# Two buffers for two output tiles and two-tap products in the tail of an SSM and gated-MLP gradient

## The chip, the cores and the metric

The kernel runs on one core of a Trainium2 chip. The metric is device time in microseconds of one execution. A profile of one execution gives the times of the single instructions. The engines are PE (matrix products; PEld is its weight load), DVE (elementwise on 128 lanes), ACT (copies out of PSUM, activations), POOL, and SP, whose queue issues nearly all DMAs. PSUM is the memory that PE writes, SBUF the one where tiles live.

## The reference

The forward pass takes `x = q` of shape (1, 2048, 512), normalises each row, and returns `x + A + B`. `A` convolves `k` with a short filter of 4 taps per channel, multiplies with `v`, runs a long causal convolution of length 2048 by FFT, and multiplies with the normalised rows. `B` is a bilinear gated MLP of hidden size 1376.

```python
def _A_ref(q, k, v, shift_k, ssm_k, ssm_D):
    for t in range(ks):
        k_shift = k_shift + k_pad[:, t:t + S, :] * shift_k[:, ks - 1 - t][None, None, :]
    kv = k_shift * v
    ...
    y = y + kv * ssm_D[None, None, :]
    return q * y
def _B_ref(x, w_gate, w_up, w_down):
    h = g * u
    return jnp.einsum("bsf,fd->bsd", h, w_down)
xn = _layernorm(x, axis=-1)
return x + _A_ref(xn, A_k, A_v, ...) + _B_ref(xn, B_w_gate, ...)
```

The kernel returns the forward result (`out_0`) and nine gradients for a given `grad_out`: of q (`out_1`), k (`out_2`), v (`out_3`), the short filter (`out_4`), the long filter (`out_5`), its skip weight (`out_6`), and the three MLP weights (`out_7` to `out_9`).

## The kernel before

A sequence of 2048 rows lies in SBUF as 128 partitions with R = 16 rows each, 512 channels (D) in bf16. The first part (to about 300 us) does the layer norm, the transforms of the long convolution and the MLP's forward and backward products over 8 chunks of 256 rows, and leaves intermediate results in DRAM (`HDD`, `GD`, `KS`, `BX`, `XN`).

The change lies in the last part. Its main loop is `dw()`, which forms the three MLP weight gradients in 11 blocks of hidden units. `down_grad(fb)` accumulates `pd` over 16 rows (L1014) and stores `od`; for the last block ACT copies one half of `od` and DVE the other, and each half is stored by its own queue (L1027). `pu` (L1050) is copied to `og` and stored (L1061). In between, `hid_t` transposes the hidden activations `hb` loaded from `HDD`; the last three blocks come through transposing DMAs instead (`natT`, L808).

Beside `dw()` run four generators, each advanced every second or third step of `dw()`:

- `inv_y()` brings 4 rows at a time back from the transform: `yC`, the convolution's result, and `dd`. From `dd`, DVE forms `dks = dd * v` (L950) and the gradient of v (L951). `dd` has two buffers in the pool `c2b`.
- `dsk_gram()` forms the gradient of the short filter as products of `dks` with shifted `k` in PSUM (`pk`), masks them with the identity into `kd` (L1079) and reduces them (L1081). A last small transpose gives `dskt`. `kd` and `dskt` have one buffer each in the pool `c2`.
- `inv_dk()` forms the gradient of the long filter, `o5t`, stored at L996.
- `ew()` walks over a list of 16 pieces: `final(0)`, `final(1)`, `bwd(0)`, `final(2)`, `bwd(1)`, ..., `final(7)`, `bwd(6)`, `bwd(7)`. Each piece works on 2 of the 16 rows, so on tiles of 128 x 1024. Before each piece, `put_late()` stores what earlier pieces left in the list `late` (L1167).

`final(b)` forms the result `o` (L1125, L1126) and the gradient of q, `e` (L1129 to L1141), with `bb` loaded from `BX` and a scratch tile `dxn` in fp32. `o`, `e` and `dxn` have one buffer each. `bwd(b)` forms the gradient of k, `dk` (two buffers), as a sum over 4 taps: products of `dks`, shifted by the tap, with the filter row `skb` (L1103, L1105), and sums (L1106). Its scratch tile `tk` shares the single buffer of `dxn`.

The order of instructions on each engine is not written out: a planner takes the operations in the order in which the program lists them as priority, works out with a cost model when each would be ready, and fixes one order for each engine and for each queue that issues DMAs. A block marked `high_priority` goes ahead when ready. An operation that needs a buffer waits until the tile before it in that buffer is done with, its store included. On the chip each engine, and the SP queue, then works strictly in that order. The PSUM tag `p2` has three buffers; `pt`, `pq`, `pu`, `pk` and `po` share them.

Of the kernel before, what the change touches and what calls it, by code (L numbers as in the profile page):

```python
# [8 lines left out]
BF = mybir.dt.bfloat16  # L9
F32 = mybir.dt.float32  # L10
I32 = mybir.dt.int32
ALU = mybir.AluOpType
# [6 lines left out]
D = 512  # L19
F = 1376  # L20
R = 16
P = 128
NC4 = 4
# [167 lines left out]
def kernel(  # L191
# [24 lines left out]
    nc = tc.nc  # L216
# [20 lines left out]
    def dve(o, i):  # L237
        nc.vector.tensor_copy(o, i)  # L238
# [13 lines left out]
    def P2(name, shape, dt=F32):  # L252
        return ps2.tile(shape, dt, name=name, tag="p2")

    def P1(name, shape, dt=F32):
        return ps1.tile(shape, dt, name=name, tag="p1")
# [5 lines left out]
    skb = const.tile([P, 4, D], BF, name="skb")  # L262
# [642 lines left out]
    c2b = ctx.enter_context(tc.tile_pool(name="c2b", bufs=2, side="right", reuse_waits="tile"))  # L905
    c2 = ctx.enter_context(tc.tile_pool(name="c2", bufs=1, side="right", reuse_waits="tile"))
    yC = c2.tile([P, R, D], BF, name="yC")
    dks = c2.tile([P, R + 3, D], BF, name="dks")
# [158 lines left out]
    def dsk_gram():  # L1067
        for c in range(NC4):
            pk = P2("pk", [P, 2, D])
            for r in range(R):  # L1070
                for h in range(2):
                    c0 = c * 128 + 64 * h
                    nc.tensor.matmul(pk[64 * h:64 * h + 64, h, 0:256], lhsT=dks[:, r, c0:c0 + 64],  # L1073
                                     rhs=KH[0][:, r:r + 4, c0:c0 + 64], start=(r == 0), stop=(r == R - 1))
            kd = c2.tile([P, 4, 64], F32, name="kd")
            with tc.high_priority(offset=SOON):
                for h in range(2):
                    hs = slice(64 * h, 64 * h + 64)
                    nc.vector.tensor_tensor(kd[hs], pk[hs, h, 0:256].rearrange("q (j c) -> q j c", j=4),  # L1079
                                            ident[hs, hs].unsqueeze(1).to_broadcast((64, 4, 64)), op=ALU.mult)  # L1080
                nc.vector.tensor_reduce(dsk[:, c, :], kd[:], axis=AX.X, op=ALU.add)  # L1081
            yield
        dskb = c2.tile([P, 4, NC4], BF, name="dskb")
        nc.vector.tensor_copy(dskb[:], dsk[:].rearrange("q c i -> q i c"))
        for _ in range(2):
            yield
        pt = P1("pts", [P, 4, P], BF)
        for j in range(4):
            nc.tensor.transpose(pt[:NC4, j, :], dskb[:, 3 - j, :], ident[:])
        dskt = c2.tile([NC4, P, 4], BF, name="dskt")  # L1090
        dve(dskt[:], pt[:NC4].rearrange("c j q -> c q j"))
        nc.sync.dma_start(out_4.rearrange("(c p) j -> c p j", p=128), dskt[:])
        yield

    def bwd(b):
        rb = slice(2 * b, 2 * b + 2)
        dk = c2b.tile([P, 2, D], BF, name="dk")
        t = c2.tile([P, 2, D], BF, name="tk", tag="dxn")
        for j in range(4):
            src = dks[:, 2 * b + j:2 * b + j + 2, :]  # L1100
            w = skb[:, j:j + 1, :].to_broadcast((P, 2, D))
            if j == 0:
                nc.vector.tensor_tensor(dk[:], src, w, op=ALU.mult)  # L1103
            else:
                nc.vector.tensor_tensor(t[:], src, w, op=ALU.mult)  # L1105
                nc.vector.tensor_tensor(dk[:], dk[:], t[:], op=ALU.add)  # L1106
        late.append((o2_n[:, rb, :], dk))

    FL = {}
# [2 lines left out]
    def load_fin(b):  # L1112
        bb = c2b.tile([P, 2, 2, D], BF, name="bb")
        nc.sync.dma_start(bb[:], BX[:, 2 * b:2 * b + 2, :, :])
        FL[b] = bb

    def final(b):
        if b + 1 < 8:
            load_fin(b + 1)
        bb = FL.pop(b)  # L1120
        rb = slice(2 * b, 2 * b + 2)
        tt = nc.vector.tensor_tensor
        stt = nc.vector.scalar_tensor_tensor
        o = c2.tile([P, 2, D], BF, name="o0")
        tt(o[:], xnC[:, rb], yC[:, rb], op=ALU.mult)  # L1125
        tt(o[:], o[:], bb[:, :, 0, :], op=ALU.add)  # L1126
        late.append((o0_n[:, rb, :], o))
        e = c2.tile([P, 2, D], BF, name="e")
        tt(e[:], goC[:, rb], yC[:, rb], op=ALU.mult)  # L1129
        dxn = c2.tile([P, 2, D], F32, name="dxn")  # L1130
        for i in range(2):
            r = 2 * b + i
            stt(dxn[:, i], e[:, i], 1.0, bb[:, i, 1, :], op0=ALU.mult, op1=ALU.add, accum_out=s1[:, r:r + 1])
            stt(e[:, i], dxn[:, i], 1.0, xnC[:, r, :], op0=ALU.mult, op1=ALU.mult, accum_out=s2[:, r:r + 1])
        nc.vector.tensor_scalar(m2[:, rb], s2[:, rb], -1.0 / D, None, op0=ALU.mult)
        stt(m1[:, rb], s1[:, rb], -1.0 / D, rstd[:, rb], op0=ALU.mult, op1=ALU.mult)
        for i in range(2):
            r = 2 * b + i
            stt(dxn[:, i], xnC[:, r, :], m2[:, r:r + 1], dxn[:, i], op0=ALU.mult, op1=ALU.add)
            nc.vector.tensor_scalar(e[:, i], dxn[:, i], rstd[:, r:r + 1], m1[:, r:r + 1], op0=ALU.mult, op1=ALU.add)  # L1140
        tt(e[:], e[:], goC[:, rb], op=ALU.add)  # L1141
        late.append((o1_n[:, rb, :], e))
# [16 lines left out]
    for b in range(8):  # L1159
        tail.append(lambda b=b: final(b))  # L1160
        if b > 0:
            tail.append(lambda b=b: bwd(b - 1))
    tail.append(lambda: bwd(7))

    def put_late():
# [16 lines left out]
    def load_dk():  # L1182
        gks.append(load_gk(0))
        gks.append(load_gk(1))
        yield

    sides = [every(seq(inv_y(), load_dk()), 0, 3), every(dsk_gram(), 27, 2), every(inv_dk(), 35, 3), every(ew(), 10, 3)]
    for n, _ in enumerate(dw()):
        for sd in sides:
# [36 lines left out]
```

## Time and profile before

| what | value |
|---|---|
| median of three runs | 489.96 us |
| lowest, highest | 488.36, 490.24 us |
| the profiled execution | 488.56 us |
| its span, first to last instruction | 486.8 us |
| mean granted PE clock | 0.995 |
| PE busy | 471.5 us (97%) |
| DVE busy | 342.0 us (70%) |
| ACT busy | 310.1 us (64%) |

The span and the time of the same execution differ by 1.8 us, which lie around it. Busy shares are means over stages of different kinds. Below, a line of a timeline gives the start, the duration, the engine (SPq is the queue of SP), the line of the kernel, the operation, the tile written and the tiles read, and their sizes.

### The profile page before, as it was taken

To read this page: it belongs to the slowest core of one execution; us is meant where nothing else is said; L and a number is where in the kernel's file an instruction comes from. 1 tells how busy PE (TensorE), PEld (TensorE's weight loads), DVE (VectorE), ACT (ScalarE), POOL (GpSimd) and SP (SyncE) were. 2 spreads that over 40 slices of the span, in tenths; PEclk is the share of its full clock that TensorE was granted. 3 is DMA by queue.
4 is the path that set the end of the run, shared out by engine and by line. 5 is a ranking of instruction groups with operands and counts; after the bars stand their busy time and mean duration, and the time that the engine had idled before them with its cause. 6 is when DMAs were issued, how large, how long until landed. Compare 5 with 4: busy or idle time off the path is not lost.

```text
span 486.8 us, 10509 instructions
## 1 busy us (share of the span) xinstructions
PE 471.5 (97%) x4335; PEld 314.8 (65%) x4335; DVE 342.0 (70%) x625; ACT 310.1 (64%) x351; POOL 13.9 (3%) x30
## 2 busy tenths in 40 slices
PE   8998999999999999999999999999999999999992
PEld 7867755547647457357357734577677778777790
DVE  7889989988275667677687874021260999998895
ACT  4956677669568678789689954567557523733320
POOL 8000000000000000000000000020000000000000
PEclk9999999999999999999999999999999999999997
DMA  8999999889999978788977199989999797999518
GB/s 266 373 366 362 314 261 359 295 314 323 306 293 284 247 235 246 240 257 250 296 231 238 63 366 324 369 314 348 342 368 373 286 354 248 316 310 231 186 48 293
DMA packets 105837, 139.87 MB, mean 287 GB/s; under 512 B 33435, under 2 KB 78912, under 8 KB 104126
## 3 DMA queue, kind: packets, MB, share of 16 engines
q1 hardware_dynamic: 104206, 137.85, 86.9%
q10 hardware_dynamic: 1584, 1.36, 1.0%
q8 instruction: 34, 0.56, 0.5%
q14 instruction: 13, 0.11, 0.1%
HBM read 68.45 MB, written 63.41 MB: 271 GB/s over the span
## 4 chain that ended last, share of the span: by engine, by line
PE 76%; DMA 11%; DVE 10%; ACT 1%; issue 1%; DVEq 0%; SPq 0%; ACTq 0%
PE px L555 14%; PE pgu L512 13%; PE pu L1050 12%; PE py L548 7%; PE pd L1014 6%; PE pdh L518 6%; PE pt L847 4%; PE pq L920 3%; PE ps L584 3%; DMA ssk<-in_A_ssm_k_dram 3%; PE pg L613 3%; PE pf L370 2%; DMA out_dram<-e 2%; DMA x_b<-in_A_q_dram 2%; PE pk L1073 2%; DMA XN<-x_b 1%
## 5 line engine op out<-in xcount | busy, mean ns | idle before, releaser
L555 PE MATMUL px<-WT,hd 128*128 128x512 bf16 (+1 forms) x352 | 81.0, 380 | 0.0
L1050 PEld LDWEIGHTS <-xnC 128*128 128x128 bf16 x704 | 67.1, 98 | 8.8 <-issue 0.9
L555 PEld LDWEIGHTS <-hd 128*128 128x128 bf16 (+1 forms) x352 | 32.8, 98 | 44.4 <-issue 7.7
L1050 PE MATMUL pu<-natd,xnC 128*128 128x256 bf16 x512 | 58.5, 273 | 0.2 <-ACT nath L235 0.2
L235 ACT CAST gu<-pgu 128x1024 bf16<-128x1024 f32 (+1 forms) x48 | 45.4, 946 | 16.5 <-PE pgu L512 16.3
L235 ACT CAST GO<-pg 128x1024 bf16<-128x1024 f32 x48 | 46.2, 1015 | 13.8 <-issue 7.2
L235 ACT CAST SP<-ps 128x1024 bf16<-128x1024 f32 x47 | 45.6, 1025 | 13.7 <-PE ps L584 11.8
L600 DVE TENSOR_TENSOR T<-SP 128x2048 bf16<-128x2048 bf16 x24 | 29.4, 1223 | 34.8 <-ACT SP L235 34.7
L512 PE MATMUL pgu<-xt,Wu 128*128 128x256 bf16 (+1 forms) x352 | 53.1, 273 | 0.7 <-DVE kn L238 0.6
L512 PE MATMUL pgu<-xt,Wg 128*128 128x256 bf16 (+1 forms) x352 | 52.8, 273 | 0.2 <-DMA Wg<-in_B_w_gate_dram 0.2
L518 PE MATMUL pdh<-gt,WdT 128*128 128x256 bf16 (+1 forms) x352 | 46.9, 273 | 0.2 <-ACT WdT L235 0.2
L235 ACT CAST fst<-pf 128x1024 bf16<-128x1024 f32 x44 | 42.7, 1030 | 5.7 <-ACT fst L235 2.1
L512 PEld LDWEIGHTS <-Wu 128*128 128x128 bf16 (+1 forms) x352 | 33.0, 100 | 15.0 <-issue 10.1
L548 PE MATMUL py<-Wd,hd 128*128 128x512 bf16 (+1 forms) x176 | 41.4, 380 | 0.0
L235 ACT COPY natd<-pt 128x2048 bf16<-128x2048 bf16 x16 | 30.0, 1874 | 14.1 <-PE pt L847 14.1
L235 ACT CAST og<-pu 128x1024 bf16<-128x1024 f32 (+1 forms) x11 | 10.9, 993 | 43.1 <-PE pu L1050 38.5
L518 PEld LDWEIGHTS <-WdT 128*128 128x128 bf16 (+1 forms) x352 | 34.8, 100 | 5.0 <-ACT WdT L235 0.4
L512 PEld LDWEIGHTS <-Wg 128*128 128x128 bf16 (+1 forms) x352 | 34.8, 100 | 4.1 <-DMA Wg<-in_B_w_gate_dram 0.5
L533 DVE TENSOR_TENSOR hd<-gu,dh 128x1024 bf16<-128x1024 bf16 (+1 forms) x48 | 30.9, 643 | 0.8
L532 DVE TENSOR_TENSOR hd<-gu 128x512 bf16<-128x512 bf16 (+1 forms) x48 | 19.1, 398 | 15.9 <-ACT gu L235 15.9
L1014 PE MATMUL pd<-goC,nath 128*128 128x512 bf16 x128 | 30.1, 379 | 0.0
L548 PEld LDWEIGHTS <-hd 128*128 128x128 bf16 (+1 forms) x176 | 16.5, 98 | 20.8 <-issue 3.1
(176 smaller groups left out, 693.2 us busy)
## 6 DMA issues: line engine op xcount, KB each, us to landing
HDD<-hd SPq DMA_DIRECT2D x35, 384.0 KB, 5.8
FD<-fst SPq DMA_DIRECT2D x24, 512.0 KB, 5.5
X<-FD SPq DMA_DIRECT2D x24, 512.0 KB, 5.2
GD<-GO SPq DMA_DIRECT2D x24, 512.0 KB, 3.9
g<-GD SPq DMA_DIRECT2D x11, 1024.0 KB, 8.7
hb<-HDD SPq DMA_DIRECT2D x8, 1344.0 KB, 7.9
bb<-BX SPq DMA_DIRECT2D x8, 512.0 KB, 6.2
BX<-bx SPq DMA_DIRECT2D x7, 512.0 KB, 3.9
```

The source lines that it names most:

```text
L235: nc.scalar.copy(o, i)
L512: nc.tensor.matmul(pgu[:w, i, t, :], lhsT=W[:, c, f0:f0 + w], rhs=xt[:, :, c, :], start=(c == 0), stop=(c == NC4 - 1))
L518: nc.tensor.matmul(pdh[:w, i, :], lhsT=WdT[:, c, f0:f0 + w], rhs=gt[:, :, c, :], start=(c == 0), stop=(c == NC4 - 1))
L532: nc.vector.tensor_tensor(hd[:fw, fb0:fb0 + n, 0, :], gu[:fw, :n, 0, :], gu[:fw, :n, 1, :], op=ALU.mult)
L533: nc.vector.tensor_tensor(hd[:fw, fb0:fb0 + n, 1:3, :], gu[:fw, :n], dh[:fw, :n].unsqueeze(2).to_broadcast((fw, n, 2, 256)), op=ALU.mult)
L548: nc.tensor.matmul(py[:], lhsT=hd[:fw, fb, 0, ss], rhs=Wd[:fw, fb, :], start=(fb == 0), stop=(fb == NFB - 1))
L555: nc.tensor.matmul(px[:], lhsT=hd[:fw, fb, t, ss], rhs=W[:fw, fb, :], start=(t == 1 and fb == 0), stop=(t == 2 and fb == NFB - 1))
L584: nc.tensor.matmul(ps[32 * q:32 * q + 32, a, :], lhsT=TB.EF[64 * a:64 * a + 64, 4 * g + q, ri].rearrange("p k j -> p (k j)"), rhs=X[64 * a ...
L600: tt(W[:].rearrange("p c a d -> p c (a d)"), A[:, i:i + 1].rearrange("p c a d -> p c (a d)").to_broadcast((P, 2, 2 * D)), B[:].rearrange(" ...
L847: nc.tensor.transpose(pt[:, r, :fw], hs[:, (r % 2) * 128:(r % 2) * 128 + 128], ident[:fw, :fw])
L1014: nc.tensor.matmul(pd[:fw, :], lhsT=nat_h(fb, r), rhs=goC[:, r, :], start=(r == 0), stop=(r == R - 1))
L1050: nc.tensor.matmul(pu[:, c, :, :fw], lhsT=xnC[:, r, cs(c)], rhs=nat_d(fb, r), start=(r == 0), stop=(r == R - 1))
```

## The change

It has three parts.

1. `o0` and `e` get two buffers each, so `final(b + 1)` can write its tiles while those of `final(b)` are still being stored. That takes two more tiles of 2 KB in each partition.
2. `kd` and `dskt`, 1 KB each, no longer have places of their own: they take turns in the two buffers of `dd`, which are also used by the last `og1`.
3. `bwd` forms the products of two taps in one operation of 2048 elements. Its source is a pattern over `dks` with two windows of two rows, the second shifted by one row, so that the middle row is read twice; the filter rows are repeated over the window. `tk` doubles to [P, 2, 2, D] in bf16, as large as `dxn`, whose buffer it shares. The four taps are summed by three additions as before.

```diff
-            kd = c2.tile([P, 4, 64], F32, name="kd")
+            kd = c2b.tile([P, 4, 64], F32, name="kd", tag="dd")
...
-        dskt = c2.tile([NC4, P, 4], BF, name="dskt")
+        dskt = c2b.tile([NC4, P, 4], BF, name="dskt", tag="dd")
...
-        t = c2.tile([P, 2, D], BF, name="tk", tag="dxn")
-        for j in range(4):
-            src = dks[:, 2 * b + j:2 * b + j + 2, :]
-            w = skb[:, j:j + 1, :].to_broadcast((P, 2, D))
-            if j == 0:
-                nc.vector.tensor_tensor(dk[:], src, w, op=ALU.mult)
-            else:
-                nc.vector.tensor_tensor(t[:], src, w, op=ALU.mult)
-                nc.vector.tensor_tensor(dk[:], dk[:], t[:], op=ALU.add)
+        t = c2.tile([P, 2, 2, D], BF, name="tk", tag="dxn")
+        for j in (0, 2):
+            s = dks[:, 2 * b + j:2 * b + j + 3, :]
+            (part, row, elem) = s.ap
+            src = bass.AP(s.tensor, s.offset, [part, [row[0], 2], [row[0], 2], elem])
+            w = skb[:, j:j + 2, :].unsqueeze(2).to_broadcast((P, 2, 2, D))
+            nc.vector.tensor_tensor(t[:], src, w, op=ALU.mult)
+            nc.vector.tensor_tensor(dk[:], t[:, 0] if j == 0 else dk[:], t[:, 1 if j == 0 else 0], op=ALU.add)
+            if j:
+                nc.vector.tensor_tensor(dk[:], dk[:], t[:, 1], op=ALU.add)
...
-        o = c2.tile([P, 2, D], BF, name="o0")
+        o = c2.tile([P, 2, D], BF, name="o0", bufs=2)
...
-        e = c2.tile([P, 2, D], BF, name="e")
+        e = c2.tile([P, 2, D], BF, name="e", bufs=2)
```

## The prediction

> **What bounds the kernel now.** I read the table of stages first (busy time of each engine in stretches that I chose), then the waits of PE, then DVE in order of time, then the sync queue at the end. In the stages, each line gives a stretch and the busy us of PE, PEld, DVE, ACT and POOL in it, the granted clock, the DMA share and GB/s:
>
> ```profile
> 360.00:380.00 20.00, 20.00 (x176) 14.94 (x174) 5.40 (x10) 11.80 (x11) 0.00 (x0) 1.00 0.99 370
> 380.00:400.00 20.00, 20.00 (x219) 15.52 (x218) 19.20 (x44) 8.33 (x7) 0.00 (x0) 1.00 0.86 298
> 400.00:420.00 20.00, 20.00 (x234) 16.16 (x232) 19.57 (x41) 9.70 (x8) 0.00 (x0) 1.00 0.88 306
> 460.00:478.00 18.00, 17.09 (x170) 14.60 (x167) 16.60 (x32) 4.75 (x6) 0.00 (x0) 1.00 0.36 132
> 478.00:486.80 8.80, 0.00 (x0) 0.00 (x0) 3.21 (x6) 0.00 (x0) 0.00 (x0) 0.70 0.84 259
> ```
>
> The reader is to see two things. PE is full at full clock until its last matmul, which starts at 476.49 and lasts 0.59, so ends at 477.08; then 9.7 us pass without it. And DVE, which this change touches, is a quarter busy from 360 to 380 and full from 380 on: it is late from then to the end. PE itself hardly waits; of PE after 300 us the list of waits has one line:
>
> ```profile
> PE pu L1050 <- ACT nath L235: 0.2, 1, 0.2
> ```
>
> DVE in order of time (start, us, instruction, and in brackets the idle time in front of it with its cause):
>
> ```profile
> 358.15 0.69 DVE L1141 TENSOR_TENSOR e<-e,goC 128x1024 bf16<-128x1024 bf16 x1
> ...
> 361.70 0.69 DVE L951 TENSOR_TENSOR kb<-dd,kb 128x1024 bf16<-128x1024 bf16 x1
> 376.91 0.69 DVE L1125 TENSOR_TENSOR o<-xnC,yC 128x1024 bf16<-128x1024 bf16 x1 [14.53 <-DMA out_dram<-o]
> ...
> 452.29 0.69 DVE L1129 TENSOR_TENSOR e<-goC,yC 128x1024 bf16<-128x1024 bf16 x1 [3.29 <-DMA out_dram<-e]
> ```
>
> So `final(1)` stands 14.53 us, with its inputs there, until the store of `final(0)`'s `o` has landed and frees the one buffer; `e` does the same later. The lateness reaches the end through the sync queue:
>
> ```profile
> 476.69 0.33 SPq L1167 DMA_DIRECT2D out_dram<-dk  x1
> 477.11 1.04 SPq L1061 DMA_DIRECT2D out_dram<-og  x2
> 478.24 1.37 SPq L996 DMA_DIRECT2D out_dram<-o5t  x2
> 481.05 0.33 SPq L1167 DMA_DIRECT2D out_dram<-dk  x1
> 481.47 1.77 SPq L1061 DMA_DIRECT2D out_dram<-og  x2
> 483.33 0.58 SPq L1027 DMA_DIRECT2D out_dram<-od  x1
> ```
>
> The queue issues in order. It stands at the store of `dk` until DVE has computed it, and the stores of `og` (whose copy on ACT began at 467.50), of `o5t` (copied by 469.42) and of the last `og` (474.47) stand behind it. DVE's half of `od` is also queued on DVE behind `bwd(7)`: it runs at 480.94, while ACT's half ran at 477.17. From the end of the last issue (483.91) to the end of the span are 2.9 us.
>
> **Part 1, two buffers for `o` and `e`.** It removes DVE's waits on their stores: 14.53 us for `o`, and 5.08 for `e` (0.59, 0.31, 3.29, 0.89 by DVE's order of time); another 1.0 us of waits for `dk`'s store stays. What is late next? `final(1)` can start at 362.3: yC's rows are there, `bb` for it was issued at 354.80 and lands 4.8 to 7.3 us later, by 362.1. From its first to its last operation `final` takes about 7.3 us of DVE (four of 0.60, four of 0.61, 1.33 and 0.92 for the two pairs, 0.2 for the small ones), `bwd(0)` behind it some 4.7. `final(2)` again needs `o`'s first buffer, whose store was issued at 365.19 and, by the 10.2 us that is the longest landing of an `o`, is down at 375.4. So of the 14.53 us, 7.3 + 4.7 = 12.0 are filled and 2.5 remain as a wait. If `e`'s 5.08 go too, DVE gains 17.1 us; if they come back as waits on the second buffer, 12.0. Nothing in the trace shows a loss here, but an idle engine in the stage 360 to 380 is also all there is to gain from: 14.6 us is the ceiling there.
>
> The stores of `final(1)` and `bwd(0)` move with it, 3 x 256 KB, into the stretch with DMA share 0.99. At that stretch's 370 GB/s they are 2.1 us of transfer, ahead of loads of `hb` that must be there for the transposes. The load issued at 366.89 took at most 13.9 us (the longest landing of an `hb`), so is down at 380.8; its transposes start on PE at 384.0. I take 0 with 3.2 us as the cover; without it, each us late is a us of PE.
>
> **Part 2, `kd` and `dskt` in `dd`'s two buffers.** The operations stay: 8 of 0.42, 4 of 0.41, one of 0.68. The new wait is on the last readers of `dd` (start 387.73, done 388.4); `kd` is first written at 393.28. That is 4.9 us of cover. Behind a late `kd` stand the three PSUM buffers of tag p2, and with them PE. `og1`, the last user of `dd`, is written at 473.67, long after `dskt`'s store (issued 433.85). Two `kd` buffers instead of one gain nothing: no wait names `kd`. I take 0; from the rows, between 0 and the 4.9 us by which `dd`'s readers could slip unnoticed.
>
> **Part 3, products of two taps in one operation.** Per `bwd` before: 4 products and 3 sums, seven operations of 1024 elements. Each of the chained ones starts 0.725 after the one before (473.00, 473.73, 474.45), the others 0.60: 0.60 + 6 x 0.725 = 4.95 alone, 7 x 0.60 = 4.2 in between other work. After: 2 products of 2048 and 3 sums. A product of 2048 with a broadcast input lasts 1.22 (T<-SP, L600), and its follower starts 1.14 later where it does not depend on it. Chained: 2 x 1.25 + 3 x 0.725 = 4.68; in between: 2 x 1.14 + 3 x 0.60 = 4.08. The gain is 0.12 to 0.27 per `bwd`, for eight 1 to 2.2 us; I take 1.6. The early start of the first product (two `dk` at 329.11, when DVE was idle) is lost, since it now needs the buffer shared with `dxn`: 2 x 0.60, so 0.4 is left.
>
> The unsure piece is the source pattern: two windows of two rows that overlap by one row. The nearest row is hd<-gu,dh, L533: three free dimensions with a repeated one, 1024 elements in 688 ns, the pace of the plain ones. I take that pace. The other bound is one element at a time, the pace of rows with fp32: 256 elements 0.42, 512 elements 0.69, so 0.27 for each 256 more, and 2048 in 2.31. It would add 2 x 1.09 to each `bwd`, 17.4 us in all. The Trainium skill, page "Vector Engine (DVE) Microarchitecture Reference", section 5.1, states that a two-source operation goes two elements per cycle when every operand is 16-bit with an innermost step of 1, and that it lists input rows that overlap among what was not measured. By its condition the sum stays 4.68 and 4.08; L533's row agrees, and no run here shows overlapping rows.
>
> **The sum.** DVE's chain: 12.0 + 5.1 + 0.4 = 17.5 us earlier at its end (12.4 if `e`'s waits come back). It ended with `bwd(7)` at 480.94; it would end at 463.4 to 468.5. All of it beyond 3.9 us lies beside PE, which ends at 477.08 as before. So the end is set by PE: ACT's half of `od` done at 477.54, DVE's at 477.6 (0.41), the sync queue free by then, its issue 0.58, and 2.9 to the end: 481.1. ACT's half was issued at 478.96, 1.4 after its copy, by a wait that the list does not name; if that stays, 479.32 + 2.9 = 482.2. I take the middle, 481.6: 5.2 less than the span of 486.8. The profiled execution took 488.56, so 483.4; the three runs have a median of 489.96, 1.4 above it, which gives 484.8. I say 484.0.
>
> **Rivals.**
> *The tail is given back in part (about 490).* The instruction order is planned anew, and every stall of PE goes straight to the end, since PE has no slack at all. A stall of 3 to 5 us takes the gain. For it: the gram's weight loads at 389.25 waited 0.21 for DVE, so PE already starts the gram at the moment `dks` is written. If DVE stands in `final(2)` then, up to 7.3 us come in front, of which some 3 hurt. Against it: `dks`' last load was issued at 377.20, lands 6.3 later, 383.5, and today's order has them late too. Time 487.5 to 492.
>
> *Slower (494).* One mechanism: the sync queue stops at a store of `e` that DVE has not yet computed, now placed further ahead, with the load of `hb` behind it. The longest such stop is 5.9 us now; one `final` and one `bwd` between two `e` make 12.0. Less the 3.2 of cover, PE stands 8.8 us; with the tail's 5.2 gained, that is 489.96 + 3.6 = 493.6. It decides from a stop of 10.8 us on (3.2 + 5.2 + 2.45). For it: the queue waited 20.6 us for `e` in all. Against it: those waits come from the lateness that goes.
>
> *The wide products run at one element per cycle.* DVE then ends 17.4 us later than forecast: at 481 instead of 463.4, or 486 instead of 468.5. The first is no change in the tail (489.96), the second 5 us more (495).
>
> **How the numbers follow.** A measurement of this kernel tells 0.5% (2.45 us) from no change. The forecast's mechanism has 0.60, with 481.5 to 487.4 as its own range; the gain given back 0.17; the queue's stop 0.15; slow products 0.08, of which half stays within 0.5% and half is slower. Faster 0.61 with a little of the given-back case, same 0.20, slower 0.19. To leave out no more than 2 in 10 the range must take in the middle case and the first of the slow ones: 481.5 to 493.
>
> **What would show it.** Right: no idle time in front of L1125 between 362 and 377; DVE's last `dk` before 472; DVE's half of `od` within 0.6 us of ACT's; the last og stores issued by 476.5; PE ending near 477; the wide product at 1.22. Wrong: PE's idle time after 300 above 3 us, with `hb`, `dd` or `dks` as its cause; a wide product near 2.3; a wait at `bb` in place of `o`'s.

## The result: faster by 1.4%

The changed kernel takes 481.98 us (median of 4 runs, 481.83 to 482.23), the kernel before 489.16 in the same comparison (median of 4). The ratio is 0.986, with a 95% interval of 0.983 to 0.989. The forecast was 484.0, faster, within 481.5 to 493.0. The profiled execution after took 482.23 us with a span of 480.4, 6.4 less than the span before.

The stages after, with the busy us of PE, PEld, DVE, ACT and POOL, the granted clock, the DMA share and GB/s:

```profile
360.00:380.00 20.00, 20.00 (x173) 14.70 (x171) 14.70 (x27) 11.80 (x11) 0.00 (x0) 1.00 0.97 360
380.00:400.00 20.00, 20.00 (x220) 15.44 (x218) 19.72 (x43) 8.32 (x7) 0.00 (x0) 1.00 0.89 322
400.00:420.00 20.00, 19.79 (x231) 15.82 (x230) 19.65 (x40) 9.16 (x8) 0.00 (x0) 1.00 1.03 371
460.00:478.00 18.00, 17.03 (x169) 14.53 (x166) 7.93 (x10) 4.74 (x6) 0.00 (x0) 1.00 0.58 196
478.00:481.00 3.00, 0.00 (x0) 0.00 (x0) 0.00 (x0) 0.00 (x0) 0.00 (x0) 0.81 0.14 33
```

From 360 to 380 DVE went from 5.40 to 14.70 us of work; from 460 to 478 from 16.60 to 7.93. PE is unchanged: 17.03 us in the second last line against 17.09. What shrank is the stretch behind PE, 9.7 us before and 3.4 now. (The last window reaches 0.6 us past the end of the span.)

DVE after in order of time, with idle time and its cause in brackets. These are the three longest waits between 360 and PE's end, the last product and sums of `bwd(7)`, and its half of `od`:

```profile
365.88 0.69 DVE L1127 TENSOR_TENSOR o<-o,bb 128x1024 bf16<-128x1024 bf16 x1 [3.07 <-DMA bb<-BX]
...
378.19 0.69 DVE L1126 TENSOR_TENSOR o<-xnC,yC 128x1024 bf16<-128x1024 bf16 x1 [1.30 <-DMA out_dram<-o]
...
452.07 0.69 DVE L1127 TENSOR_TENSOR o<-o,bb 128x1024 bf16<-128x1024 bf16 x1 [4.02 <-DMA bb<-BX]
...
465.17 1.23 DVE L1104 TENSOR_TENSOR tk<-dks,skb 128x2048 bf16<-128x2048 bf16 x1
466.43 0.69 DVE L1105 TENSOR_TENSOR dk<-dk,tk 128x1024 bf16<-128x1024 bf16 x1
467.16 0.69 DVE L1107 TENSOR_TENSOR dk<-dk,tk 128x1024 bf16<-128x1024 bf16 x1
477.51 0.42 DVE L238 CAST od<-pd 96x256 bf16<-96x256 f32 x1 [9.66 <-ACT od L235]
```

The wait of 14.53 us is gone. From 360 to PE's end the waits on stores went from 20.6 us (14.5 for `o`, 5.1 for `e`, 1.0 for `dk`) to 1.3, and in their place come three waits on loads of `bb`, 7.7 us together (the third, of 0.58, is not shown). `bwd(7)` ends at 467.85, 13.2 us earlier than the 481.02 of before, and DVE then stands idle for 9.66 us until the last `pd` is there.

PE's last matmul, ACT's half of `od`, and the sync queue at the end, after:

```profile
476.44 0.59 PE L1014 MATMUL pd<-goC,nat 128*96 128x512 bf16 x2
477.11 0.37 ACT L235 CAST od<-pd 96x256 bf16<-96x256 f32 x1 [2.70 <-PE pd L1014]
...
468.48 0.93 SPq L1061 DMA_DIRECT2D out_dram<-og  x2
469.50 1.17 SPq L996 DMA_DIRECT2D out_dram<-o5t  x2
470.77 1.19 SPq L1168 DMA_DIRECT2D out_dram<-dk  x1
474.44 1.31 SPq L1061 DMA_DIRECT2D out_dram<-og  x2
477.96 0.34 SPq L1027 DMA_DIRECT2D out_dram<-od  x1
```

None of them stands behind late work of DVE any more: `dk`, done at 467.85, itself waits its turn behind `og` and `o5t`, and the last `og` (copied by 474.41) and `od` (477.93) are issued as soon as their copies are done. The last issue ends at 478.30, and 2.1 us later the span ends.

### The profile page after: what moved, and what is told of

Its sections match the earlier page's. It is cut to its first block, busy times and chain, and to the rows that moved or that the text cites. A ratio compares the mean times of both kernels' runs of the same rounds, so it can differ in the third digit from the quotient of the medians.

```text
span 480.4 us, 10491 instructions
## 1 busy us (share of the span) xinstructions
PE 471.0 (98%) x4335; PEld 314.3 (65%) x4335; DVE 340.1 (71%) x609; ACT 310.3 (65%) x351; POOL 13.9 (3%) x30
## 4 chain that ended last, share of the span: by engine, by line
PE 74%; DMA 14%; DVE 10%; ACT 1%; issue 1%; SPq 1%; ACTq 0%; DVEq 0%
PE px L555 15%; PE pgu L512 13%; PE pu L1050 11%; PE py L548 7%; PE pdh L518 6%; PE pd L1014 6%; PE ps L584 3%; PE pf L370 3%; DMA khC<-in_A_k_dram 3%; DMA ssk<-in_A_ssm_k_dram 3%; PE pg L613 3%; PE pt L847 2%; DMA vb<-in_A_v_dram 2%; DMA kb<-KS 2%; DMA x_b<-in_A_q_dram 2%; PE pq L920 1%
```

## The experiments

Theory A: DVE's lateness, begun at the wait in front of `final(1)` and passed on by the sync queue, set the end; the buffers remove it, and PE's end then sets the time. Theory B: the wider products give the gain. Theory C, formed on the way: the store that `final(1)` waits for lands late because the 2.4 MB load of `khC` was issued ahead of it. Twelve kernels ran; a ratio stands against the kernel before in the same comparison, with its 95% interval.

| kernel | median us | before us | ratio (interval) |
|---|---|---|---|
| buffers, no merged products | 481.93 | 490.18 | 0.9836 (0.9795 to 0.9876) |
| merged products only | 487.86 | 490.18 | 0.9958 (0.9931 to 0.9986) |
| two buffers for `o` only | 491.96 | 490.18 | 1.0046 (1.0016 to 1.0077) |
| two buffers for `e` only | 482.95 | 490.18 | 0.9846 (0.9806 to 0.9887) |
| first stores ahead of `khC` | 488.13 | 489.16 | 0.9977 (0.9955 to 0.9999) |
| changed, first products twice | 484.07 | 489.16 | 0.9906 (0.9878 to 0.9933) |
| changed, all products twice | 487.10 | 489.16 | 0.9959 (0.9938 to 0.9980) |
| changed, one tap of four | 481.63 | 489.16 | 0.9858 (0.9835 to 0.9880) |
| small tiles moved only | 489.42 | 489.61 | 0.9998 (0.9967 to 1.0029) |
| last `od` on ACT | 488.54 | 489.61 | 0.9985 (0.9958 to 1.0012) |
| `e` in front of `o` | 490.45 | 489.61 | 1.0026 (1.0000 to 1.0051) |
| `e`'s buffer and merged products | 482.45 | 489.61 | 0.9860 (0.9820 to 0.9901) |

### The parts one at a time

The first: the changed kernel with the old products.

```diff
-            kd = c2.tile([P, 4, 64], F32, name="kd")
+            kd = c2b.tile([P, 4, 64], F32, name="kd", tag="dd")
...
-        o = c2.tile([P, 2, D], BF, name="o0")
+        o = c2.tile([P, 2, D], BF, name="o0", bufs=2)
...
-        e = c2.tile([P, 2, D], BF, name="e")
+        e = c2.tile([P, 2, D], BF, name="e", bufs=2)
```

> The changed kernel with the k gradient's products left as before, one tap each. Theory A (the buffers end DVE's lateness, and PE's end at 477.0 sets the time): DVE's last operation of bwd(7) ends 1 to 2.5 us later than the 467.85 of the changed kernel, at about 470, still in front of PE's end, so the time is that of the changed kernel, 482.0 within 0.5. Theory B (the wider products give a good part of the gain, the buffers only exchange a wait on a store for a wait on bb): 485 or more.

481.93: as A expected, and B falls. DVE's `bwd(7)` ended at 467.86, and not 1 to 2.5 us later as I had set for the narrow products; its waits on `bb` are 14.0 us here and 15.9 with the wide products. The buffers alone give the whole gain, as far as these runs can tell.

Then the merged products on the kernel before, `bwd` as in the change and nothing else:

```diff
-        t = c2.tile([P, 2, D], BF, name="tk", tag="dxn")
-        for j in range(4):
...
+        t = c2.tile([P, 2, 2, D], BF, name="tk", tag="dxn")
+        for j in (0, 2):
...
```

> The kernel before with the wide products alone. Theory A: the waits on the stores of o (14.5 us) and e (5.1 us) stay, DVE ends 1 to 2.2 us earlier than its 480.9, and since the sync queue and DVE's half of od stand behind it the time falls by as much: 487.0 to 488.3 against 489.2. Theory B: 482 to 485.

487.86, 2.3 us less, in A's range. In the profiled executions DVE's `bwd(7)` ends 1.2 us earlier (479.86 against 481.02), and since the last stores stand behind it, the span falls with it, from 486.8 to 485.2. Beside the buffers the same saving is worth nothing.

Then kd and dskt alone:

```diff
-            kd = c2.tile([P, 4, 64], F32, name="kd")
+            kd = c2b.tile([P, 4, 64], F32, name="kd", tag="dd")
...
-        dskt = c2.tile([NC4, P, 4], BF, name="dskt")
+        dskt = c2b.tile([NC4, P, 4], BF, name="dskt", tag="dd")
```

> The kernel before with kd and dskt moved to dd's buffers and nothing else. Theory A (only a way to find room): no wait appears at kd, the time is that of before, between 0.997 and 1.003 of it. Rival (kd waits for dd's readers and PE for kd): PE's waits for kd above 3 us, 492 or more.

0.9998. The order of instructions is the same on every engine, and no wait names `kd`; the part buys room and costs nothing. It is needed: without it the two new tiles have no room in SBUF.

### Which buffer

```diff
-        o = c2.tile([P, 2, D], BF, name="o0")
+        o = c2.tile([P, 2, D], BF, name="o0", bufs=2)
```

> The kernel before with two buffers for o alone (2 KB, which fit without moving kd and dskt). Theory A: final(1) no longer waits for o's store but for that of e, issued 0.4 us later at 365.6 and landing in about 4, so it begins at about 370 instead of 376.9: 7 of the 14.5 us are gained, DVE ends at about 474, in front of PE's 477, and nearly all of the gain is there: 482 to 483.5. Rival: both buffers are needed, the wait moves whole from o to e: 488 or more.

491.96, slower than before by 0.46%. A's 482 to 483.5 falls; the rival's number holds, but the wait did not move to `e`. DVE in order of time in this kernel:

```profile
366.94 0.69 DVE L1126 TENSOR_TENSOR o<-o,bb 128x1024 bf16<-128x1024 bf16 x1 [2.93 <-DMA bb<-BX]
379.62 0.69 DVE L1125 TENSOR_TENSOR o<-xnC,yC 128x1024 bf16<-128x1024 bf16 x1 [11.99 <-DMA out_dram<-o]
380.30 0.69 DVE L1129 TENSOR_TENSOR e<-goC,yC 128x1024 bf16<-128x1024 bf16 x1
```

The first line is `final(1)` finishing its `o` in the second buffer. The next is already the `o` of `final(2)`, which the planner has put in front of the `e` of `final(1)`. It waits 11.99 us for the store of the first `o`, and `final(1)`'s long part, which begins with `e`, waits behind it. DVE is no less late than before (its `bwd(7)` ends at 483.88, 2.9 us later), and now PE is late too. (The profiled execution, 494.17, is 2.2 us above this kernel's median.) PE's waits in this kernel (line, releaser, us in total, times, longest):

```profile
PE pt L847 <- DVE kd L1079: 3.2, 2, 2.0
PE pt L847 <- DMA hb<-HDD: 0.6, 1, 0.6
```

The transposes stand for a PSUM buffer that `kd` frees, and `kd` stands on DVE behind other work: one `o` waited 2.04 for `bb` at 415.94, and `kd` came at 419.92. PE's last matmul ends at 481.83, 4.8 us later than before.

```diff
-        e = c2.tile([P, 2, D], BF, name="e")
+        e = c2.tile([P, 2, D], BF, name="e", bufs=2)
```

> The kernel before with two buffers for e alone. Theory A: the wait of 14.5 us at o stays as it is, the 5.1 us at e go, DVE ends at about 476, just in front of PE's end: 482.5 to 485. Rival (o's buffer is what counts): 487.5 or more.

482.95 with a ratio of 0.9846, the whole gain within the intervals. It is in A's range, but not for A's reason. The expectation let the 14.5 us at `o` stand. DVE in this kernel:

```profile
363.87 0.69 DVE L1133 SCALAR_TENSOR_TENSOR dxn<-e,bb 128x512 f32<-128x512 bf16 x1 [1.99 <-DMA bb<-BX]
369.62 0.68 DVE L1105 TENSOR_TENSOR tk<-dks,skb 128x1024 bf16<-128x1024 bf16 x1
...
376.15 0.69 DVE L1125 TENSOR_TENSOR o<-xnC,yC 128x1024 bf16<-128x1024 bf16 x1 [2.22 <-DMA out_dram<-o]
```

With `e` free, the planner runs `e` of `final(1)` early, its long part from 363.87 and `bwd(0)` from 369.62, and puts the `o` of `final(1)` behind them. `o` still has one buffer and still waits for the same store, which is free at about 376 as before, but only 2.22 us of that wait are left.

The last of these has two buffers for `e` and the merged products, and one buffer for `o`:

```diff
-        e = c2.tile([P, 2, D], BF, name="e")
+        e = c2.tile([P, 2, D], BF, name="e", bufs=2)
...
-        t = c2.tile([P, 2, D], BF, name="tk", tag="dxn")
-        for j in range(4):
...
+        t = c2.tile([P, 2, 2, D], BF, name="tk", tag="dxn")
+        for j in (0, 2):
...
```

> The kernel before with two buffers for e and the wide products; o with one buffer, kd and dskt where they were. Theory A (e's second buffer carries the gain, o's is not needed): DVE ends in front of PE's 477, and the time is that of the changed kernel, 482.0 within 0.8. Rival (o's second buffer has a part in it): 484 or more.

482.45, ratio 0.9860 as for the whole change: `o`'s second buffer has no part that these runs can tell.

### Why the store was late, and whose wait it was

The stores of `final(0)` are issued ahead of `khC`'s load:

```diff
+        put_late()
-        with tc.issue_after(LG["g"].ins):
+        with tc.issue_after(LG["late"].ins):
             nc.sync.dma_start(khC[:, 3:3 + R, :], k_n)
...
-            nc.sync.dma_start(dst, t[:])
+            LG["late"] = nc.sync.dma_start(dst, t[:])
```

> The kernel before, single buffers, but the stores of final(0)'s o and e are issued ahead of the 2.4 MB load of khC instead of behind it. Theory C (o's store landed late, 10 us after its issue, because that load was issued in front of it): o's store lands in 4 to 5 us, by about 368, final(1) begins 8 to 9 us earlier than 376.9, DVE ends at 472 to 473, in front of PE's end, and the time is 482 to 484. Rival (the store is slow for another reason, or khC's load is then late for the gram on PE at 389): 487 or more.

488.13, the rival's side by the time, with a ratio of 0.9977 whose interval ends just under 1. (The profiled execution, 486.11, is 2.0 us below this median.) The sync queue and then DVE in this kernel:

```profile
362.73 0.61 SPq L1168 DMA_DIRECT2D out_dram<-o  x1
363.39 0.42 SPq L1168 DMA_DIRECT2D out_dram<-e  x1
363.85 0.82 SPq L1151 DMA_DIRECT2D khC<-in_A_k_dram  x1
...
389.94 1.31 SPq L785 DMA_DIRECT2D g<-GD  x2
391.35 0.80 SPq L1168 DMA_DIRECT2D out_dram<-o  x1
```

```profile
369.72 0.69 DVE L1125 TENSOR_TENSOR o<-xnC,yC 128x1024 bf16<-128x1024 bf16 x1 [8.03 <-DMA out_dram<-o]
...
403.99 0.69 DVE L1125 TENSOR_TENSOR o<-xnC,yC 128x1024 bf16<-128x1024 bf16 x1 [3.48 <-DMA out_dram<-o]
...
450.63 0.69 DVE L1129 TENSOR_TENSOR e<-goC,yC 128x1024 bf16<-128x1024 bf16 x1 [4.17 <-DMA out_dram<-e]
```

Theory C's local claim holds, if not its 4 to 5 us: from issue to the operation that waited are 7.0 us, against 11.7 before (365.19 to 376.91). DVE starts `final(1)` 7.2 us earlier, of which 2.5 come from the earlier issue and 4.7 from the faster store. The faster store agrees with the Trainium skill, page "DMA: Bandwidth & Descriptors", section "Queues, rings and completion order", by which each DMA engine takes the descriptors of a queue in ring order. But with single buffers DVE waits again: all its waits on stores from 385 on are 9.0 us against 6.1 before, and 1.2 for `vb` come in. The wait of 3.48 has the form of the one that was removed: the store it waits for is issued at 391.35 right behind two loads of `g`, 1 MB each, and takes 12.6 us to land, the longest of any `o` in this kernel. `bwd(7)` ends at 478.39, 2.6 us earlier and not 8. A wait shortened once came back at a later store behind a large load.

Next comes the kernel before with `o`'s two operations behind the last of `e`:

```diff
-        tt(o[:], xnC[:, rb], yC[:, rb], op=ALU.mult)
-        tt(o[:], o[:], bb[:, :, 0, :], op=ALU.add)
...
-        tt(e[:], e[:], goC[:, rb], op=ALU.add)
+        done = tt(e[:], e[:], goC[:, rb], op=ALU.add)
+        with tc.issue_after(done.ins):
+            tt(o[:], xnC[:, rb], yC[:, rb], op=ALU.mult)
+        tt(o[:], o[:], bb[:, :, 0, :], op=ALU.add)
```

> The kernel before, single buffers, with the two operations of o put behind the last operation of e in each final, so that the first thing that final(1) waits for is the store of e and not that of o. Theory C (both stores lie behind khC's load and land together): e's store, issued at about 366, lands at 376 to 377, final(1) begins at 377 as before, 487 to 491. Rival (e's store lands in about 4 us, as its other stores do, and the wait was o's alone): final(1) begins at 370, DVE ends at 474, 482 to 484.

490.45, as C expected. DVE in this kernel:

```profile
377.98 0.69 DVE L1125 TENSOR_TENSOR e<-goC,yC 128x1024 bf16<-128x1024 bf16 x1 [16.41 <-DMA out_dram<-e]
```

The store of `e`, issued at 364.85, is down at 378, no sooner than that of `o`. So before the change both waits were there, one over the other, and the profile named `o` because `o` stood first on DVE.

### How much cover DVE has

In the changed kernel, the product of the first two taps is formed twice:

```diff
             nc.vector.tensor_tensor(t[:], src, w, op=ALU.mult)
+            if j == 0:
+                nc.vector.tensor_tensor(t[:], src, w, op=ALU.mult)
```

> The changed kernel with the first wide product of each bwd formed twice, 8 operations of 1.25 us more on DVE, 10 us. Theory A (DVE ended 9.2 us in front of PE, and this cover is free): DVE's last operation of bwd(7) ends at 474 to 478, the time is 482.0 to 483. Rival (DVE still sets the time somewhere): 487 or more.

484.07, in between: `bwd(7)` ended at 473.31, still in front of PE, and yet the time rose by 2 us over the changed kernel. Of PE's weight loads the list of waits has this line, where the changed kernel has 0.9:

```profile
PEld L847 <- DVE kd L1079: 1.9, 1, 1.9
```

PE's last matmul ended at 478.12 instead of 477.03, and the profiled executions differ by about as much (483.25 and 482.23). The cover at the end was free, the one at the gram was not. For the second us between the medians no trace was kept.

Then each product twice:

```diff
             nc.vector.tensor_tensor(t[:], src, w, op=ALU.mult)
+            nc.vector.tensor_tensor(t[:], src, w, op=ALU.mult)
```

> The changed kernel with both wide products of each bwd formed twice, 16 of 1.25 us, 20 us more on DVE, some 3 more than products at one element per cycle would have cost. Theory A: some 4 us are absorbed in the wait for bb, DVE ends at 484 to 488, 7 to 11 behind PE's 477, and the time is 5.9 + 1.8 behind DVE's end, as it was before the change: 491.5 to 495.5. Rival (PE bounds all, DVE's work is free): 482.

487.10, far below A's 491.5. The end of DVE and of the sync queue in this kernel:

```profile
480.08 0.69 DVE L1108 TENSOR_TENSOR dk<-dk,tk 128x1024 bf16<-128x1024 bf16 x1
480.69 0.41 DVE L238 CAST od<-pd 96x256 bf16<-96x256 f32 x1
```

```profile
475.32 1.15 SPq L996 DMA_DIRECT2D out_dram<-o5t  x2
480.80 0.33 SPq L1169 DMA_DIRECT2D out_dram<-dk  x1
481.22 0.99 SPq L1061 DMA_DIRECT2D out_dram<-og  x2
482.30 0.48 SPq L1027 DMA_DIRECT2D out_dram<-od  x1
```

DVE's busy time rose by 18.8 us (340.2 to 359.0), its end by 12.9 (467.85 to 480.77). Waits for `bb` fell from 15.9 to 9.6 us; 1.7 of that lies at `final(0)`, in front of all the added work, so 4.6 us of added work went into these waits. And the span ends 4.4 us behind DVE instead of the 5.8 of before. That goes with `o5t`, which was stored at 475.32 and not 478.24, and with the last `og` pair, whose issue took 0.99 us and not 1.77; the cause was not tested.

The other way, the k gradient cut to one tap (three of the four taps are left out):

```diff
-        t = c2.tile([P, 2, 2, D], BF, name="tk", tag="dxn")
-        for j in (0, 2):
...
+        nc.vector.tensor_tensor(dk[:], dks[:, rb, :], skb[:, 0:1, :].to_broadcast((P, 2, D)), op=ALU.mult)
```

> The changed kernel with the k gradient cut to its first tap: each bwd is one operation, 32 us less on DVE; three of the four taps are left out of out_2. Theory A (PE's end sets the time, the tail behind it is 3.4 us): 481.5 to 482.3, as the changed kernel. Rival (DVE or the sync queue still holds PE or the end back): 480 or less.

481.63 against 481.98: 29.5 us less busy time on DVE (340.2 to 310.6) are worth nothing that can be told from no change. PE's end and the tail behind it are the floor.

### What held the end before

```diff
-            for h, cp, q in ((0, act, nc.scalar), (1, dve, nc.sync)):
+            for h, cp, q in ((0, act, nc.scalar), (1, act, nc.scalar)):
```

> The kernel before with both halves of the last od copied by ACT and stored from ACT's queue, so that the end no longer waits for od behind DVE's bwd(7). Theory A (the sync queue, standing at dk's store, holds back og as well): the last og stores are issued as late as before, by 483.2, and only the issue of od behind them goes: 0.5 to 1 us less, 488.2 to 488.9 against 489.2. Rival (the copy of od on DVE alone made the late end): 484 to 485.

488.54, in A's range, though the interval (0.9958 to 1.0012) takes in no change. The rival's 484 falls: `od` behind DVE was not what held the end. The last `og` still stand behind the last `dk` in the sync queue, although ACT had copied them by 473.87:

```profile
478.11 0.33 SPq L1167 DMA_DIRECT2D out_dram<-dk  x1
478.54 1.93 SPq L1061 DMA_DIRECT2D out_dram<-og  x2
```

(This profiled execution, 485.98, is the fastest of the twelve, 2.6 us below the median; its `bwd(7)` ended at 478.08.)

## Why the prediction was right, and where it was not

**The end.** Right. PE ended at 477.03 (forecast 477.08), DVE's half of `od` ran 0.4 us behind ACT's, and the last `og` was issued by 475.75. The one-tap kernel shows the floor. The terms that were mis-sized are the last ones: 0.58 for the issue and 2.9 for the landing, both taken from an end with a DMA share near 1, measured 0.34 and 2.1 with a share of 0.14. Against that, DVE's half waited for ACT's (477.51, `<-ACT od`), which the sum, with both halves starting at 477.17, did not have: 0.35 us. The unnamed wait of 1.4 us of ACT's store, of which the sum took half, was not there (issued at 477.51). So the span is 480.4 and not 481.6. The prediction's own steps from the span give 484.8, and for the 484.0 that it states it gives no reason. The time is 482 because the span fell by 6.4 and not by 5.2, and because the profiled execution after lies 0.25 above its median, where the one before lay 1.4 below the median of the three runs then known.

**Part 1.** Right in size, in part by luck (the waits that came back are somewhat longer than the lower bound had them, and stand at another place), and wrong in its division. DVE's end came 13.2 us earlier, inside the 12.4 to 17.5. But the division, "14.53 us for `o`, and 5.08 for `e`", failed. `e` alone gives the whole gain and `o` alone a loss: the two stores land at nearly the same time, and which operation stands in front of DVE at that time decides. What came next was not a wait on the second buffer, as the lower bound had it, but on `bb`, named only under what would make the prediction wrong: 15.9 us in four waits against 6.6 in one before, and from 360 on 7.7 against none. Of `final(1)`'s inputs, `bb` was to land by 362.1; issued at 355.36, it let DVE go on at 365.88. For the time at which `o`'s first buffer is free the prediction has two values: 375.4, from the longest landing in the list, and 376.9, by which it gets the 2.5 us of wait that remain. Its own line for DVE shows the second: that store, issued at 365.19, let DVE go on 11.7 later. After the change it is 11.5 (366.69 to 378.19). `final(1)` went on 3.6 us later than forecast, the buffer came free 1.3 later, and 1.30 of wait remained.

**Part 2.** Right: no cost, shown alone. In the kernel with the buffers and no merged products, where `kd` is moved too, no wait names `kd` either.

**Part 3.** Right as work: the wide product lasts 1.20 to 1.23, and a chained `bwd` takes 4.66 (463.19 to 467.85), forecast 4.68. The unsure pattern runs at full pace; the condition of the Trainium skill, page "Vector Engine (DVE) Microarchitecture Reference", section 5.1, thus also holds here for input rows that overlap, which it lists as not measured. Worth nothing beside the buffers, 0.42% without them.

**The rivals.** The price of products at one element per cycle was too high: it took DVE's end to move with the added work and the tail behind it to stay. With 20 us added, 487.1 was measured, where 17.4 had been priced at 490 to 495. The slower rival (the sync queue stopping ahead of `hb`) did not come; the loss that the `o`-only kernel shows has, by its waits, mostly another path, named in Part 2: `kd` late on DVE, the PSUM buffers held, PE standing. In the changed kernel weight loads wait 0.9 us on that path and matmuls 0.2; in the kernels with `e`'s buffer alone, with and without merged products, nothing waits for `kd`, and PE ends at 476.40 and 476.51 instead of 477.03.

What stays open: why the planner's order, with two buffers for `o`, puts the third `o` in front of the second `e` was read from the order only. In the early-store kernel the wait of 3.48 follows a store behind two large loads; the one of 4.17 for `e` was not taken apart. And no run let `og` and `od` go ahead of the last `dk` in the sync queue, so how much of the 5.8 us behind DVE is the order in that queue, and how much DVE's own late end, was not separated.

## What to carry to other kernels

A wait names the operation that stands first on its engine, not the only one that would have to wait: before giving a tile a second buffer, look which of the tiles behind it are held by the same transfer, and try the buffer first on the one whose chain is longest. Where an engine in order is late at the end, count what stands behind its stores in the issuing queue; that, and not its own work, may be the tail. A saving on such an engine counts only until the next engine's end is reached, and added work is partly absorbed by the waits that it had.

## What was not expected of the hardware

A store of 256 KB behind a load of 2.4 MB in the same queue took 11.7 us until the operation that waited for it could start, and 7.0 when issued in front of it. With a DMA share of 0.14 at the end, the last small store took 2.1 us from the end of its issue to the end of the span, with a share near 1 it took 2.9. How far the runs of one kernel lie apart does not follow DVE's place at the end alone: where DVE ends in front of PE they lie within 0.4 us (the changed kernel, four runs) to 3.6 (first products twice, six runs).
